# A causal attention with two gated MLPs on one core: when the planner ranks twelve small rows, and whether it holds small VectorE steps back for GpSimd

## The chip, the cores and the metric

The kernel runs on one core of one Trainium2 chip. The metric is the device time of one execution in microseconds (us); of several executions the median counts. Engines are called PE (TensorE), DVE (VectorE), ACT (ScalarE), POOL (GpSimd) and SP (SyncE, which here only issues DMAs).

## The reference, cut to what matters

Three stages in float32: an attention over 4 batches of 8 heads with 576 positions of 64 elements, and two gated MLPs ("MoE") over the 2304 tokens that come out of it. The first of these begins with an RMS normalisation.

```python
cum = np.cumsum(np.maximum(s, 0.0), axis=-1)
bias = -(cum[:, :, :, None] - cum[:, :, None, :])
scores = np.where(causal, -1e9, scale * q @ k.T + np.minimum(bias, 0.0))
attn = exp(scores - max) / (sum + 1e-09)
x = (attn @ v), heads side by side           # 2304 x 512
xn = x / sqrt(mean(x * x) + 1e-06) * rms_g
h = (silu(xn @ w_gate) * (xn @ w_val)) @ w_out     # 512 -> 1536 -> 512
out = (silu(h @ w2_gate) * (h @ w2_val)) @ w2_out
```

## The kernel before, in words

**A planner writes the order.** The program never issues an instruction when it meets it. Every operation is put down with `op(engine, ns, fn, r=, w=, pri=, later=, port=)`: engine, estimated duration, what it reads and writes, a rank and two options. `Plan.run` then plays the whole list through a model and gives each engine its order: of the operations ready at a time, the one with the lowest `pri` goes first. On the chip every engine works through its own queue strictly in that order, and waits where something it needs isn't there yet.

Two options matter here. `later=1000` makes an operation ready 1000 ns (in the model) after the engines' work that it depends on. `port=True`, on a DVE operation, models SBUF ports that DVE and GpSimd share: such an operation isn't started in the model while a GpSimd operation runs there, and the reverse (L203 and L236). These are rules of the plan; on the chip nothing but semaphores and the hardware holds an instruction back. In the model SP is busy 450 ns with a small DMA, and about 1500 ns with a 512 KB one.

**The early attention.** The first 256 positions (group "A") of batches 0 and 1 are computed first, as sixteen small units, one for each head (`EarlyUnit`, i = 0 to 15, called head 0 to head 15 below; the first eight are those of batch 0). A unit loads q and k of its head in one DMA of 128 KB (L879), its values in one of 64 KB (L891), multiplies q by k (L899), finds the least of each row on DVE (L690), takes the exponent on ACT (L701), transposes it (L917) and multiplies by the values (L927). The bias by the cumulated s is a matmul of its own for units 0 to 3 (L905). For units 4 to 15 it is an added row of k: a DMA of 1 KB (L884) copies one row of the cumulated s (`cumA`) below k in the unit's tile, `lq`. Two tiles with two halves each serve all sixteen, so unit i can load only when the scores of unit i - 4 are done. All three loads have rank i - 1000 and go through SP's queue.

In the same queue stand the weights of the first MLP: 512 KB for each half of a hidden block f (L434, `raw<-in_w_gv`), with rank -992 + 1.5 f. They are turned into two fp32r halves by ACT (L438, L445), DVE (L440, L449) and POOL (L446, L449).

**The early normalisations.** When all eight heads of a batch are in x, `normalise(..., split=False)` runs for its 256 tokens: squares on ACT (L958), their sums on PE (L965), then 20 small steps on DVE, each a line `step(...)` from L1020 to L1054: the division by the softmax's sums, the mean, an inverse root by three Newton rounds of three steps (L1035, L1037, L1038), and the factors' two halves. Each step needs the one before it. Two transposes (L1058), a copy (L1061) and four spreading matmuls (L1066) follow, then x is scaled (L1070), split (L1073, L1075), and the gate matmuls of the first MLP (L1086) can begin. These have a rank far behind (10,000), so that the planner uses them to fill PE wherever the attention has nothing ready. The later normalisations, of the rest of the batches, call the same function with `split=True`.

**Behind it** come the remaining attention (group "B" and batches 2 and 3), with the first MLP's matmuls between, and then the two output layers and the second MLP.

Of the kernel before, what the change touches and what calls it, by code (L numbers as in the profile page):

```python
# [40 lines left out]
PE, DVE, ACT, POOL, SP, NONE = "PE", "DVE", "ACT", "POOL", "SP", "NONE"  # L41
# [38 lines left out]
class Plan:  # L80
# [20 lines left out]
    def op(self, eng, ns, fn, r=(), w=(), pri=0.0, later=0, port=False, slow=0.0):  # L101

        n = len(self.ops)
        done = 0
        if eng == SP:  # L110
            took = ns / self.RATE
            ns = max(450.0, took)
            done = 2300.0 + took - ns + slow
        deps, shared = set(), []
        for accesses, writes in ((r, False), (w, True)):
            for a in accesses:
                buf, part = a if isinstance(a, tuple) else (a, None)
                key = buf if isinstance(buf, str) else buf.key
                live = self.live.setdefault(key, [])
                keep = []  # L120
                for part2, m, wrote in live:
                    meets = part is None or part2 is None or part == part2
                    if meets and (writes or wrote) and m != n:
                        deps.add(m)
                    if not (writes and meets and (part is None or part == part2)):
                        keep.append((part2, m, wrote))
                keep.append((part, n, writes))
                self.live[key] = keep
                if not isinstance(buf, str) and buf.share is not None and buf not in shared:
                    shared.append(buf)  # L130
                    buf.uses += 1
        engs = eng if isinstance(eng, list) else [(eng, ns)]
        self.ops.append((engs, fn, deps, pri, done, shared, later, port))
        return n
# [160 lines left out]
TINY = 70  # L295
# [5 lines left out]
def tile_kernel(  # L301
# [16 lines left out]
    op = plan.op  # L318
# [10 lines left out]
    def buf(pool, tag, shape, dtype, name=None):  # L329
        return Buf(f"{pool}.{tag}",  # L330
                   lambda: pools[pool][1].tile(shape, dtype, name=name or tag, tag=tag))
# [143 lines left out]
    cumA = buf("at", "pTB1", [P, 2 * P], F32, "cumA")  # L475
# [100 lines left out]
    class Head:  # L576
# [13 lines left out]
        def load(self, pri):  # L590
            b, h, n, nv = self.b, self.h, self.n, self.nv
            i = b * NH + h
            c0 = self.c0
            q0, k0, c0_ = lq_parts(self.ql, 0)
            q1, k1, c1_ = lq_parts(self.ql, 1)
            self.qp, self.kp = [k0, k1], [q0, q1, c0_, c1_]
            op(SP, 4 * P * n, lambda en: en.dma_start(
                out=self.ql()[:, :n], in_=qk[b, h, :, 1, :n]), w=self.kp, pri=pri, later=2500)
            op(SP, 4 * D * (QW - c0), lambda en: en.dma_start(
                out=self.ql()[:D, S + c0:], in_=qk[b, h, :D, 0, c0:]),  # L600
               w=self.qp, pri=pri, later=2500)
            op(SP, 4 * P * n, lambda en: en.dma_start(
                out=self.cb()[:, :n], in_=cum_d[i:i + 1, :n].to_broadcast([P, n])),
               r=["cum_d"], w=[self.cb], pri=pri, later=2500)
            op(SP, 256 * P * nv, lambda en: en.dma_start(out=self.vl()[:, :nv], in_=vp[b, h, :, :nv]),
               w=[self.vl], pri=pri, later=2500)
# [241 lines left out]
    class EarlyUnit(Unit):  # L848
# [28 lines left out]
        def load(self, pri):  # L877
            ql, i = self.ql
            op(SP, 8 * D * 256, lambda en: en.dma_start(  # L879
                out=ql()[0:D, :, 288 * i:288 * i + 256], in_=qk[self.b, self.h, 0:D, :, 0:256]),  # L880
               w=self.parts[:2], pri=pri)
            n = self.b * NH + self.h
            if not self.first:
                op(SP, 1024, lambda en: en.dma_start(  # L884
                    out=ql()[D:D + 1, 1, 288 * i:288 * i + 256], in_=cumA()[n:n + 1]),
                   r=[cumA, self.rows], w=self.parts[2:], pri=pri, later=1000)
            if self.first:
                op(ACT, 450, lambda en: en.dma_start(
                    out=self.v(), in_=vp[self.b, self.h, :, 0:2]), w=[self.vl], pri=pri - 1e6)
            else:  # L890
                op(SP, 512 * P, lambda en: en.dma_start(  # L891
                    out=self.v(), in_=vp[self.b, self.h, :, 0:2]), w=[self.vl], pri=pri)
# [47 lines left out]
    def normalise(i, g, tot, pri, split=True):  # L940
# [15 lines left out]
        for k in range(KD):  # L956
# [3 lines left out]
               r=[(x, (k, 0)), (x, (k, 64))], w=[q], pri=pri)  # L960

            if not split:
# [14 lines left out]
                op=ALU.subtract), r=[q, qh], w=[sqL], pri=pri, port=True)  # L977
# [6 lines left out]
        if split:  # L984
# [3 lines left out]
               r=[ps], w=[sq[0]], pri=pri)  # L988
            ps2 = mo_bank()
            for c in range(nt):  # L990
                op(PE, C_TR, lambda en, c=c: en.transpose(
                    ps2()[:, c * P:c * P + P], sq[0]()[:, at[c]:at[c] + P], ident()),
                   r=[sq[0], ident], w=[ps2], pri=pri)
# [3 lines left out]

        def step(fn, r=(), w=None):
            w = [col] if w is None else w
            op(DVE, TINY, fn, r=[*w, *r], w=w, pri=pri, port=True)  # L1000

        def m():
            return col()[:, 0, :nt]
# [13 lines left out]
        def u():  # L1017
            return fac()[:, 1, :nt]
        F, U = (fac, 0), (fac, 1)
        step(lambda en: en.tensor_scalar(out=over(), in0=tot()[:, :nt], scalar1=1.0e-9,  # L1020
                                         scalar2=None, op0=ALU.add), [tot], [F])
        step(lambda en: en.reciprocal(over(), over()), [], [F])
        step(lambda en: en.tensor_tensor(out=u(), in0=squares(), in1=over(), op=ALU.mult),
             [ps, F], [U])
        step(lambda en: en.tensor_tensor(out=u(), in0=u(), in1=over(), op=ALU.mult), [F], [U])
        step(lambda en: en.tensor_reduce(out=m(), in_=u(), axis=mybir.AxisListType.X,
                                         op=ALU.add), [U])
# [6 lines left out]
        for _ in range(3):  # L1034
# [8 lines left out]
            op=ALU.mult), [col], [F])  # L1043
# [7 lines left out]
        def columns(z):  # L1051
# [3 lines left out]
                                         op=ALU.subtract), [F], [rr])  # L1055
        tp = mo_bank()
        for c in range(nt):
            op(PE, C_TR, lambda en, c=c: en.transpose(  # L1058
                tp()[:, at[c]:at[c] + P], rr()[:, c * P:c * P + P], ident()), r=[rr, ident], w=[tp],
               pri=pri)  # L1060
        op(ACT, c_act(n), lambda en: en.activation(rT(), tp()[:, :n], ACTF.Copy),  # L1061
           r=[tp], w=[last], pri=pri)
        for k in range(KD):
# [10 lines left out]
               r=halves, w=[(H, k)], pri=pri)  # L1074
            op([(POOL, c_ptt(n)), (DVE, c_tt(n))], 0, lambda en, k=k: en.tensor_tensor(  # L1075
                out=L()[:, k, :n], in0=x()[:, k, :n], in1=f32(H()[:, k, :n]), op=ALU.subtract),
               r=halves + [(H, k)], w=[(L, k)], pri=pri, port=True)
# [56 lines left out]
    later = setup()  # L1134
# [767 lines left out]
```

## Time and profile before

| | |
|---|---|
| median of 3 runs | 1056.55 us (1056.55, 1058.98, 1052.65) |
| profiled execution, device time | 1057.39 us |
| its span, first to last instruction | 1055.6 us |
| mean granted clock of PE, of full speed | 0.997 |
| PE busy | 1040.2 us (99%) |
| DVE, ACT, POOL busy | 771.7 (73%), 641.5 (61%), 273.5 us (26%) |

All stretches and rows are of that one profiled execution, and their times count from the start of its span; 1.8 us of the device time lie around the span. A share of busy time is an average over stages. PE's clock has two levels, 2.4 GHz (1.00) and 1.2 GHz (0.50).

### The profile page before, as it was taken

How to read it: one execution, taken by the hardware profiler on the slowest of the kernel's cores; microseconds unless marked ns; L12 is line 12 of the kernel's file. 1: busy time of each engine (PE TensorE's matmuls, PEld its weight loads, DVE VectorE, ACT ScalarE, POOL GpSimd, SP SyncE). 2: the span in 40 equal slices, each digit the busy share in tenths (PEclk: the TensorE clock that was granted, in tenths of full speed). 3: DMA queues.
4: the chain of work that ended last, by engine and by line, in shares of the span. 5: the costliest groups of instructions: out<-in, count | busy, mean ns of one | idle time of the engine just before them, and what ended most of it. 6: DMA issues, size and time to landing. Idle time of an engine off the chain costs nothing.

```text
span 1055.6 us, 19496 instructions
## 1 busy us (share of the span) xinstructions
PE 1040.2 (99%) x6322; PEld 937.2 (89%) x6322; DVE 771.7 (73%) x1880; ACT 641.5 (61%) x1373; POOL 273.5 (26%) x370
## 2 busy tenths in 40 slices
PE   8899999999999999999999999999999999999998
PEld 6599999999999999999988889888888888888888
DVE  7699788777777776757779887665667766976462
ACT  6689778867664775333466865555556444665652
POOL 4368556544343542000000000212122221300000
PEclk9899999999999999999999999999999999999999
DMA  7797555534546732666697662666667667888673
GB/s 204 229 282 221 144 150 148 164 117 128 158 142 204 246 106 85 188 208 206 206 299 244 197 222 84 222 210 220 228 202 256 219 232 263 292 259 261 207 244 105
DMA packets 127959, 211.17 MB, mean 200 GB/s; under 512 B 16176, under 2 KB 55600, under 8 KB 127856
## 3 DMA queue, kind: packets, MB, share of 16 engines
q1 hardware_dynamic: 126656, 209.32, 62.8%
q8 instruction: 50, 0.82, 0.3%
q10 hardware_dynamic: 1200, 0.60, 0.2%
q14 instruction: 53, 0.43, 0.1%
HBM read 145.29 MB, written 64.56 MB: 199 GB/s over the span
## 4 chain that ended last, share of the span: by engine, by line
PE 79%; DMA 7%; DVE 6%; ACT 3%; issue 3%; POOL 1%; SPq 1%; ACTq 0%; POOLq 0%; DVEq 0%
PE mo L1086 21%; PE mo L1455 8%; PE mo L1626 8%; PE sps L1626 6%; PE tp L1455 6%; PE sps L1455 5%; PE tp L745 4%; PE tp L733 3%; PE sps L664 2%; PE mo L1702 2%; DMA raw<-in_w_gv 2%; PE sps L1086 2%; PE tp L1086 2%; PE mo L1510 2%; DMA lq<-cumA 1%
## 5 line engine op out<-in xcount | busy, mean ns | idle before, releaser
L1086 PE MATMUL mo<-xL,H 128*128 128x256 f32 (+1 forms) x672 | 201.8, 300 | 0.1
L1086 PE MATMUL mo<-xH,H 128*128 128x256 f32 (+1 forms) x672 | 200.7, 300 | 0.3
L1086 PE MATMUL mo<-xH,L 128*128 128x256 f32 (+1 forms) x672 | 200.2, 298 | 0.0
L1351 DVE TENSOR_TENSOR hL<-hh,hH 128x512 fp32r<-128x512 f32 (+1 forms) x192 | 125.2, 662 | 67.1 <-ACT hH L1348 66.4
L1348 ACT ACTIVATE hH<-hh 128x512 fp32r<-128x512 f32 (+1 forms) x192 | 115.2, 603 | 91.6 <-DVE hL L1351 21.3
L1086 PEld LDWEIGHTS mo<-xL,H 128*128 128x128 f32 x672 | 127.0, 189 | 1.0 <-POOL xL L1075 0.5
L1086 PEld LDWEIGHTS mo<-xH,H 128*128 128x128 f32 x672 | 126.7, 189 | 1.1 <-ACT xH L1073 0.6
L1086 PEld LDWEIGHTS mo<-xH,L 128*128 128x128 f32 x672 | 126.9, 189 | 0.2
L701 ACT ACTIVATE sc<-sc,col 128x128 f32<-128x128 f32 (+3 forms) x128 | 73.2, 572 | 48.4 <-DVE col L690 46.1
L1455 PE MATMUL mo<-hH,wo 128*128 128x512 f32 x312 | 97.8, 389 | 0.0
L1455 PEld LDWEIGHTS mo<-hH,wo 128*128 128x128 f32 x312 | 58.6, 188 | 12.2
L1455 PE MATMUL mo<-hL,wo 128*128 128x512 f32 x156 | 61.1, 391 | 0.2 <-DVE hL L1351 0.2
L1455 PE MATMUL tp<-hH,wo 128*128 128x512 f32 x192 | 60.4, 389 | 0.0
L1093 ACT ACTIVATE t<-mo 128x256 f32<-128x256 f32 (+1 forms) x84 | 33.9, 403 | 43.4 <-PE mo L1086 43.3
L1632 ACT ACTIVATE u<-sps 128x512 f32<-128x512 f32 x48 | 28.5, 593 | 50.6 <-PE sps L1626 48.8
L745 PE MATMUL tp<-pTB,vst 128*128 128x320 f32 (+2 forms) x320 | 52.2, 294 | 1.6 <-ACT pTB L736 1.0
L1455 PE MATMUL sps<-hH,wo 128*128 128x512 f32 x168 | 52.9, 389 | 0.0
L1095 DVE SCALAR_TENSOR_TENSOR t<-t,mo 128x256 f32<-128x256 f32 (+1 forms) x84 | 37.8, 450 | 19.4 <-ACT t L1093 19.1
L738 DVE TENSOR_TENSOR pTB<-tp,pTB 128x512 fp32r<-128x512 f32 x64 | 44.0, 687 | 8.3 <-ACT pTB L736 7.2
L745 PEld LDWEIGHTS tp<-pTB,vst 128*128 128x128 f32 x320 | 46.5, 189 | 3.6 <-ACT pTB L736 1.7
L1589 POOL TENSOR_TENSOR tmp<-x,x 128x512 f32<-128x512 f32 x2 | 2.9, 1454 | 178.5 <-DVE x L1471 178.5
L733 PE MATMUL tp<-ident,sc 128*128 128x128 f32 x304 | 46.9, 274 | 0.6 <-DVE x L754 0.4
(289 smaller groups left out, 2925.9 us busy)
## 6 DMA issues: line engine op xcount, KB each, us to landing
raw<-in_w_gv SPq DMA_DIRECT2D x44, 511.8 KB, 5.4
tb<-h_d SPq DMA_DIRECT2D x48, 256.0 KB, 3.9
t<-tb SPq DMA_DIRECT2D x48, 256.0 KB, 2.4
hh<-t SPq DMA_DIRECT2D x48, 256.0 KB, 3.1
lq<-in_qk SPq DMA_DIRECT2D x32, 288.0 KB, 3.6
cb<-cum_d SPq DMA_DIRECT2D x32, 288.0 KB, 3.9
hh<-h_d SPq DMA_DIRECT2D x36, 256.0 KB, 3.6
h_d<-hh SPq DMA_DIRECT2D x54, 128.0 KB, 2.3
```

What stands on the lines that cost most here:

```text
L701: op(ACT, c_act(o + m, 2) + 35, lambda en: en.activation(sc()[:m, :o + m], sc()[:m, :o + m], ACTF.Exp, scale=-1.0, bias=col()[:m, 0, t:t + 1],
L733: op(PE, C_TR, lambda en, pt=pt, a=a, kb=kb, t=t: en.transpose(pt()[:, a * P:a * P + P], self.sc[t]()[:, kb * P:kb * P + P], ident()), r=[ ...
L738: op(DVE, c_tt(n), lambda en, pt=pt, c=c: en.tensor_tensor(out=place(L, c), in0=source(pt, c), in1=f32(place(H, c)), op=ALU.subtract), r=[ ...
L745: op(PE, c_mm(n), lambda en, w=w, z=z, kb=kb, d0=d0, n=n, o=o: en.matmul(po()[:, o:o + n], vst[j]()[:, kb, :], pT[g][z]()[:, d0:d0 + n], s ...
L1086: op(PE, c_mm(n), lambda en, a=a, x=x, c=c, k=k, i=i: en.matmul(ps()[:, :n], a()[:, c], x()[:, k, :n], start=(k == 0 and i == 0), stop=(k ...
L1093: op(ACT, c_act(n), lambda en: en.activation(t()[:, :n], gp()[:, :n], ACTF.Tanh, scale=0.5), r=[gp], w=[t], pri=pri)
L1095: op(DVE, c_tt(n), lambda en: en.scalar_tensor_tensor(out=t()[:, :n], in0=t()[:, :n], scalar=1.0, in1=gp()[:, :n], op0=ALU.add, op1=ALU.mu ...
L1348: op(ACT, c_act(n) + 35, lambda en: en.activation(H(), src(), ACTF.Copy), r=[src, *after], w=[H], pri=pri)
L1351: lambda en: en.tensor_tensor(out=L(), in0=src(), in1=f32(H()), op=ALU.subtract),
L1455: op(PE, c_mm(n), lambda en, m=m, w=w, xx=xx, kk=kk, i=i: en.matmul(ps[m]()[:, :n], w(), xx(), start=first and kk == 0 and i == 0, stop=kk ...
L1626: op(PE, c_mm(n), lambda en, w=w, xx=xx, cut=cut, kk=kk, i=i: en.matmul(ps()[:, :n], W[w]()[:, cut], xx(), start=first and kk == 0 and i == 0,
L1632: op(ACT, c_act(n), lambda en: en.activation(dst(), ps()[:, :n], ACTF.Copy), r=[ps], w=[dst], pri=-1.0e4)
```

## The change

Two lines. The row of the cumulated s gets a rank three lower than the other loads of its unit, so that in SP's queue it stands as the loads of the unit three before it do. The small steps of a normalisation are put down with `port=split`: for the two early ones, where `split` is False, the planner no longer keeps them and GpSimd's operations apart; for the others nothing changes. What is computed is the same.

```diff
@@ class EarlyUnit: load @@
             if not self.first:
                 op(SP, 1024, lambda en: en.dma_start(
                     out=ql()[D:D + 1, 1, 288 * i:288 * i + 256], in_=cumA()[n:n + 1]),
-                   r=[cumA, self.rows], w=self.parts[2:], pri=pri, later=1000)
+                   r=[cumA, self.rows], w=self.parts[2:], pri=pri - 3, later=1000)
@@ def normalise @@
         def step(fn, r=(), w=None):
             w = [col] if w is None else w
-            op(DVE, TINY, fn, r=[*w, *r], w=w, pri=pri, port=True)
+            op(DVE, TINY, fn, r=[*w, *r], w=w, pri=pri, port=split)
```

## Rows read from the trace of the kernel before

**Rows 1.** Waits of PE, first 90 us: total, times, longest (us).
```profile
PE sps L899 <- DMA lq<-cumA: 3.5, 2, 2.5
```

**Rows 2.** Stretches: length, then each engine's busy us (instructions), granted clock, DMA share, GB/s.
```profile
0.00:38.30 38.30, 32.08 (x178) 23.22 (x179) 28.12 (x111) 26.67 (x80) 15.93 (x31) 1.00 0.74 202
38.30:60.00 21.70, 20.55 (x117) 16.02 (x118) 16.43 (x47) 15.79 (x41) 7.30 (x8) 0.84 0.82 260
60.00:75.00 15.00, 14.69 (x116) 14.19 (x116) 13.96 (x48) 13.42 (x32) 11.77 (x13) 1.00 0.90 280
```

**Rows 3.** The same view, finer, around the longest wait (order: PE PEld DVE ACT POOL).
```profile
35.80:38.30 2.50, 0.03 (x1) 0.02 (x1) 0.63 (x2) 1.22 (x3) 1.48 (x2) 1.00 0.67 205
38.30:40.00 1.70, 1.69 (x7) 1.70 (x8) 0.30 (x2) 0.49 (x2) 0.00 (x0) 0.50 0.86 232
...
42.00:44.00 2.00, 2.00 (x9) 1.46 (x7) 0.77 (x4) 0.39 (x2) 1.90 (x2) 0.50 0.20 39
44.00:45.50 1.50, 1.50 (x6) 0.68 (x5) 0.43 (x2) 1.00 (x5) 0.04 (x1) 0.63 0.69 205
```

**Rows 4.** Timeline of SP's queue: start, us, line, what is issued.
```profile
28.82 0.57 SPq L434 DMA_DIRECT2D raw<-in_w_gv  x1
29.48 0.38 SPq L891 DMA_DIRECT2D vl<-in_vp  x1
29.91 0.43 SPq L434 DMA_DIRECT2D raw<-in_w_gv  x1
30.38 0.55 SPq L879 DMA_DIRECT2D lq<-in_qk  x1
31.33 0.33 SPq L891 DMA_DIRECT2D vl<-in_vp  x1
31.70 0.56 SPq L884 DMA_DIRECT2D lq<-cumA  x1
```

**Rows 5.** DMAs issued from 29.9 to 32.25 us: size, us to landing.
```profile
raw<-in_w_gv SPq DMA_DIRECT2D x1, 511.8 KB, 7.1
lq<-in_qk SPq DMA_DIRECT2D x1, 128.0 KB, 7.3
...
lq<-cumA SPq DMA_DIRECT2D x1, 1.0 KB, 6.5
```

**Rows 6.** Timeline of PE: start, us, line, tiles [idle before, releaser].
```profile
26.89 0.68 PE L899 MATMUL sps<-lq 128*128 128x256 f32 x2
...
30.43 0.86 PE L927 MATMUL tp<-pTA,vl 128*64 128x256 f32 x4
...
40.72 1.54 PE L927 MATMUL tp<-pTA,vl 128*64 128x256 f32 x4
...
46.68 0.86 PE L927 MATMUL tp<-pTA,vl 128*64 128x256 f32 x4 [0.65 <-DVE pTA L923]
...
51.24 0.57 PE L1086 MATMUL mo<-xH,H 128*128 128x256 f32 x2
52.31 0.44 PE L917 MATMUL tp<-ident,sc 128*128 128x128 f32 x2 [0.49 <-ACT sc L701]
```

**Rows 7.** Timeline of DVE: three small steps of the first normalisation.
```profile
30.22 0.17 DVE L1023 TENSOR_TENSOR fac<-mo,fac 128x16 f32<-128x16 f32 x1
...
35.10 0.16 DVE L1038 SCALAR_TENSOR_TENSOR rc<-rc 128x2 f32<-128x2 f32 x1
...
41.17 0.15 DVE L1035 SCALAR_TENSOR_TENSOR rc<-rc 128x2 f32<-128x2 f32 x1
```

**Rows 8.** Tile rc, first 95 us: duration in ns (least/median/most), first and last start.
```profile
L1037 DVE TENSOR_TENSOR rc<-rc x6: 142/156/973, 33.3 to 86.3; 128x2 f32<-128x2 f32 x6
L1038 DVE SCALAR_TENSOR_TENSOR rc<-rc x6: 148/162/835, 33.5 to 86.6; 128x2 f32<-128x2 f32 x6
...
L1028 DVE TENSOR_SCALAR rc<-rc x2: 155/700/1245, 32.0 to 66.7; 128x2 f32<-128x2 f32 x2
```

**Rows 9.** The same view of tile fac.
```profile
L1054 DVE TENSOR_TENSOR sq<-fac,sq x2: 177/224/270, 48.1 to 91.1; 128x16 f32<-128x16 f32 x2
```

## The prediction

> **What bounds the kernel now.** I read the share of busy time first: TensorE (PE) is busy 1040.2 of 1055.6 us, so only its 15.4 us of idle time, and stretches at a low granted clock, can be won. Next the table of stretches [rows 2]: 6.2 us of that idle time lie before 38.3 us, 1.15 between 38.3 and 60, 0.3 between 60 and 75. Both edits touch work that ends by 91.4 us (the last small step, L1054 [rows 9]), so what lies behind can change only because the planner orders it anew.
>
> Then the waits of PE [rows 1]: the longest in the first 90 us, 3.5 us in two pieces, ends with a row of the cumulated s landing (lq<-cumA); the larger piece is 2.5 us. The stretches around it [rows 3] show PE busy 0.03 of 2.5 us up to 38.3, and then the granted clock at 0.50 (1.2 GHz instead of 2.4) until 44 and 0.63 on average until 45.5, which puts the rise near 45.1. The smaller piece, 1.0 us, was followed by no fall: in the table the clock before 38.3 is 1.00.
>
> So one stall costs twice. What the clock costs: 6.8 us at half speed would lose 3.4 us if all work followed the clock; four value matmuls (L927) took 1.54 us at the low clock against 0.86 at the full one [rows 6], which makes it 6.8 x (1 - 0.86/1.54) = 3.0. I take 3.2. Stall and clock together are 5.7 us, 0.54% of the time.
>
> **Edit 1, the row ranked three heads ahead.** No DMA is added: 12 rows (heads 4 to 15 of the first sixteen) change their place in SP's queue. Each needs the cumulated s, long there, and the scores of the head four before it; in the planner it is ready 1000 ns after those. The two late rows differ.
>
> Head 4's (the 1.0 us piece): its old rank, -996, already beat the weight transfer issued before it (-990.5), so only its ready time put it behind, and the new rank alters nothing there. Gain 0.
>
> Head 13's: SP's order [rows 4] is weight half at 28.82, values of head 11, weight half at 29.91, q and k of head 13 at 30.38, values of head 12 at 31.33, the row at 31.70. Head 9's scores end at 27.5 (26.89 + 0.68 [rows 6]), so on that clock the row is ready near 28.6, before the second weight half. The old rank, -987, stands behind that half (-987.5) and both values (-989, -988); the new one, -990, beats all three. I expect it at about 29.4, in front of 512 KB of weights, and landed near 33, about as the transfers issued before it.
>
> But the scores of head 13 need its q and k too, and these keep rank -987. They were issued at 30.38 and landed 7.3 us later, at 37.7; the row landed at 31.70 + 6.5 = 38.2 [rows 5]. Between them lie only 0.5 us. With the row out of the way the next late one is this 128 KB transfer, behind the same two weight halves. The stall shrinks from 2.5 to 2.0 us, not to nothing: gain 0.5. The bounds: all of it, 2.5, if the new order also puts q and k before the second half; 0, if SP's 450 ns for the row let the values of head 12 become ready first. They outrank q and k and wait until 31.3 for head 8's value matmuls (30.43 + 0.86 [rows 6]); q and k would then be issued where the row is now and land near 38.2. I take 0.5, the difference of the two landings as they stand.
>
> Displaced in SP's queue are values of heads up to three back, by one issue (0.55 us). Head 11's are issued at 29.48 and used at 40.72 [rows 4, 6], so this is hidden; the cover is some 7 us and ends only if a value transfer slips behind two more weight halves.
>
> The clock: an idle time of 1.0 us left it at 2.4 GHz, one of 2.5 us was followed by 1.2. The 2.0 us that I expect to remain lie between, nearer to the fall. Bounds 0 and 3.2; I take a third of the price, 1.1, because the executions shown before differ by 6.3 us (1052.65 to 1058.98), so that a step of this size may be absent in some already.
>
> **Edit 2, the small steps.** An early normalisation has 20 steps on VectorE (DVE). The planner set one only where GpSimd (POOL) was idle in the plan; now it doesn't look. No instruction is added.
>
> First normalisation: 12 steps from L1023 at 30.22 to the end of the second Newton round at 35.26 take 5.0 us, 0.42 each with other work between; the next comes only at 41.17 [rows 7], the last at 48.1 (L1054 [rows 9]), since in that order they stand behind GpSimd's conversions and behind head 13's scores. Unheld, the six left would take 6 x 0.42 = 2.5 us and end near 37.8 to 38. From the last step to the first gate matmul (L1086, 51.24) are 3.2 us, so the MoE's matmuls could start near 41 instead of 51 and fill gaps behind that: 0.65 us before the value matmuls at 46.68 and 0.49 at 52.31 [rows 6]. Sum 1.1. All idle time from 38.3 to 75 is 1.15 + 0.3 = 1.45, the upper bound; the lower is a loss (third rival). They come too late for the stall itself: it begins at 35.8, before the chain ends, and PE takes its instructions in order.
>
> Second normalisation: its 18 steps from L1023 on fall after 60, where PE is busy 14.69 of 15 us and DVE 13.96 [rows 2]. To end earlier frees more MoE work there, and little is idle: gain 0.
>
> The Trainium skill has a rule against this edit (SBUF — State Buffer, "Who interferes with whom"): a DVE operation in a two-port mode, or with two SBUF inputs against a GpSimd operation that reads SBUF, fully blocks until the one that came first is done. The trace agrees: L1028 took 1245 ns at worst against 155 at best [rows 8].
>
> **The sum.** 1057.4 (the profiled execution) - 0.5 - 1.1 - 1.1 = 1054.7. The median of the runs shown lies 0.8 below that execution, so as a median 1053.9; own range of this case 1051.5 to 1056.5. A kernel of this spread can't tell 0.5% (5.3 us) from no change, so this case is "the same".
>
> **Rivals.**
> 1. The stall goes entirely, clock and all: 1057.4 - 2.5 - 3.2 - 1.1 = 1050.6, as a median 1049.8. For it: 2.5 us less at the head of a chain that PE follows for the next 7 us. Against it: q and k landing at 37.7. Needed is that the new plan lifts these over a weight half too, or that early MoE matmuls come into PE's order before head 13's scores. Chance 0.2.
> 2. The row doesn't move, or q and k take its late place: only the filled gaps remain, 1057.4 - 1.1 = 1056.3, median 1055.5. For it: a margin of SP's order of about one issue. Chance 0.2.
> 3. Slower: the second normalisation's steps meet GpSimd on its ports. Between 60 and 75 GpSimd is busy 11.77 of 15 us, 78% [rows 2]. Three steps there already ran 1.09, 0.81 and 0.67 us over their best (L1028, L1037, L1038 [rows 8]), 2.6 together. Packed into that stretch, 18 steps x 0.78 x half of 1.09 us make 7.7, that is 5.1 more (bounds: 0, and 18 x 1.09 = 19.6). DVE has 15 - 13.96 = 1.0 us free, so 4.1 us fall on its other work, the scores' minima and weight conversions. It decides only where PE runs out of MoE matmuls whose weights are converted. If all reaches PE and nothing of edit 1 is won: 1057.4 + 4.1 = 1061.5, median 1060.7. Against it: PE's 0.3 us of idle time there shows work in store. Chance 0.13.
>
> **How the numbers follow.** Forecast 0.47, rivals 0.2, 0.2, 0.13. Faster by over 0.5% (below 1051.3): three quarters of rival 1 and a tenth of the forecast and of rival 2, 0.22. Slower by over 0.5% (above 1061.8): half of rival 3 and a little of rival 2, where a new order of all later work goes badly, 0.09. The same: 0.69. The range goes from rival 1's time to rival 3's, 1049.6 to 1060.5.
>
> **What would show it.** Head 13's row issued before the weight half and landed by 34, and PE's wait before head 13's scores ending with lq<-in_qk instead of lq<-cumA, near 37.7: step 1 right. A wait that still ends with the row, or no wait, shows it wrong. A granted clock of 1.00 all through 38 to 46, and the gain nears rival 1. L1054 before 39 and the first L1086 before 43 show edit 2 right; small steps over 1 us in number, with PE waiting for DVE after 60, show rival 3. What would make the whole wrong: a new wait behind 100 us, where the order changes too without my having priced it.

## The result: 0.8% slower, where 0.25% faster was forecast

| | before | after |
|---|---|---|
| median of 6 runs each | 1054.17 us (1052.41 to 1058.98) | 1063.93 us (1061.26 to 1065.93) |
| ratio | | 1.0082, 95% interval 1.0056 to 1.0107 |
| profiled execution, its span | 1057.39, 1055.6 us | 1065.05, 1063.3 us |
| PE busy, idle in the span | 1040.2, 15.4 us | 1043.7, 19.6 us |

The three runs added on the side of before pulled its median down by 2.4 us: the profile that the prediction was read from is one of its slower executions. Of the 7.7 us between the two spans, 4.2 are idle time of PE; the other 3.5 are busy time for the same 6322 matmuls, so idle time, which the rows below go by, is not the whole loss. Times below are ratios to runs of the kernel before on the same chip, since its median moved between 1053 and 1056 us from one set of runs to another.

**The early stall.** After: waits of PE up to 100 us (total, times, longest), where [rows 1] had 3.5 us ending with the row.

```profile
PE sps L899 <- DMA vl<-in_vp: 2.6, 2, 2.1
PE sps L664 <- DVE rc L1035: 1.3, 1, 1.3
...
PE mo L1066 <- DVE hh L1098: 1.0, 1, 1.0
PE sps L899 <- DMA lq<-in_qk: 0.6, 1, 0.6
...
PE mo L1058 <- DVE sq L1054: 0.5, 1, 0.5
```

SP's queue after, as in [rows 4] (start, us, line, what is issued):

```profile
31.13 0.43 SPq L434 DMA_DIRECT2D raw<-in_w_gv  x1
31.66 0.55 SPq L884 DMA_DIRECT2D lq<-cumA  x1
32.31 0.53 SPq L891 DMA_DIRECT2D vl<-in_vp  x1
32.88 0.42 SPq L434 DMA_DIRECT2D raw<-in_w_gv  x1
33.40 0.50 SPq L884 DMA_DIRECT2D lq<-cumA  x1
33.99 0.53 SPq L891 DMA_DIRECT2D vl<-in_vp  x1
34.58 1.25 SPq L879 DMA_DIRECT2D lq<-in_qk  x2
```

Counted from head 4, the row at 31.66 is head 13's and the first transfer at 34.58 its q and k. The row now stands ahead of a weight half, with four other issues between it and its own q and k. It is issued at 31.66, as late as before (31.70), and lands some 3 us earlier, near 35.3; q and k land 5.0 us behind their issue (7.3 in [rows 5]). DMAs issued from 31.6 to 32.25 us, and from 34.5 to 35.9 (the second line is of two transfers):

```profile
lq<-cumA SPq DMA_DIRECT2D x1, 1.0 KB, 3.6
lq<-in_qk SPq DMA_DIRECT2D x2, 128.0 KB, 5.0
```

PE's wait before head 13's scores ends with q and k:

```profile
15.11 0.46 PE L899 MATMUL sps<-lq 128*128 128x128 f32 x2 [2.08 <-DMA vl<-in_vp]
...
39.79 0.89 PE L899 MATMUL sps<-lq 128*128 128x128 f32 x4 [0.62 <-DMA lq<-in_qk]
...
44.86 0.42 PE L1086 MATMUL mo<-xH,H 128*128 128x256 f32 x2
```

That is PE's timeline, as in [rows 6]. The wait is 0.62 us where [rows 3] had 2.5, and the first gate matmul starts at 44.86 instead of 51.24. But head 13's scores start 1.5 us later than before (39.79, against 38.31 where the wait of [rows 3] ends): PE comes late to the place, after a wait of 2.08 us for head 4 and a fall of the granted clock behind that, from 16.0 to 19.4 us (third line). At the old place the clock stays up (stretches as in [rows 3]):

```profile
35.80:38.30 2.50, 2.29 (x14) 1.31 (x12) 2.30 (x13) 2.16 (x7) 0.31 (x1) 1.00 0.92 255
38.30:40.00 1.70, 1.08 (x10) 1.02 (x10) 1.67 (x6) 1.59 (x4) 1.62 (x2) 1.00 0.98 261
17.00:19.00 2.00, 2.00 (x7) 1.48 (x6) 0.91 (x5) 1.50 (x6) 0.25 (x1) 0.50 0.15 36
```

**Where the time went instead.** The same three stretches of three profiles, in this order: before, after, and a second execution of the kernel before (b2 below). First number: length; second: PE busy.

```profile
0.00:55.00 55.00, 47.62 (x258) 34.70 (x258) 39.95 (x150) 37.51 (x110) 20.91 (x36) 0.94 0.76 221
55.00:110.00 55.00, 54.35 (x427) 52.57 (x426) 51.78 (x160) 49.67 (x118) 42.65 (x52) 1.00 0.79 245
110.00:235.00 125.00, 124.81 (x953) 123.20 (x953) 99.03 (x364) 95.17 (x242) 69.11 (x111) 1.00 0.49 142
```

```profile
0.00:55.00 55.00, 49.73 (x284) 37.71 (x285) 42.20 (x149) 40.71 (x118) 21.80 (x40) 0.97 0.77 223
55.00:110.00 55.00, 51.47 (x395) 49.09 (x394) 51.17 (x148) 46.32 (x106) 38.08 (x47) 1.00 0.77 235
110.00:235.00 125.00, 122.15 (x916) 118.74 (x916) 101.30 (x352) 93.07 (x234) 62.17 (x103) 1.00 0.49 136
```

```profile
0.00:55.00 55.00, 49.49 (x287) 36.94 (x288) 44.45 (x156) 41.29 (x118) 22.31 (x38) 1.00 0.81 235
55.00:110.00 55.00, 54.30 (x430) 53.13 (x430) 51.06 (x165) 47.43 (x114) 42.35 (x54) 1.00 0.80 240
110.00:235.00 125.00, 124.81 (x952) 123.37 (x951) 97.76 (x357) 95.86 (x244) 67.87 (x110) 1.00 0.50 144
```

Up to 55 us the changed kernel is ahead of the first profile of before (284 matmuls to 258), but not of the second (287). From 55 to 235 PE is idle 3.53 + 2.85 = 6.4 us after, 0.84 and 0.89 before. The instruction counts say it again: between 110 and 235 PE got through 916 matmuls instead of 953. The part between 60 and 75 us that [rows 2] showed nearly full has PE busy 12.17 of 15 us now:

```profile
60.00:75.00 15.00, 12.17 (x91) 11.38 (x91) 14.76 (x49) 10.71 (x26) 9.76 (x12) 1.00 0.79 260
```

There the second normalisation's steps stand close together. DVE after (start, us, line):

```profile
60.39 1.06 DVE L1030 TENSOR_SCALAR rc<-rc 128x2 int32<-128x2 int32 x1
...
61.74 1.22 DVE L1032 TENSOR_SCALAR rc<-rc 128x2 int32<-128x2 int32 x1
...
65.19 1.08 DVE L1038 SCALAR_TENSOR_TENSOR rc<-rc 128x2 f32<-128x2 f32 x1
66.19 0.34 DVE L690 CUSTOM_DVE_ANT_0 sc<-sps,sc,col 128x128 f32<-128x128 f32 x1
66.46 0.08 DVE L690 DVE_READ_ACCUMULATOR2_ANT col<- 128x1 f32 x1
66.46 0.15 DVE L1035 SCALAR_TENSOR_TENSOR rc<-rc 128x2 f32<-128x2 f32 x1
```

and GpSimd's operation there, and PE behind them:

```profile
64.95 1.30 POOL L449 TENSOR_TENSOR L<-raw,H 128x512 fp32r<-128x512 f32 x1 [2.02 <-ACT H L445]
...
66.69 0.41 PE L664 MATMUL sps<-kHH,qst 128*128 128x384 f32 x1 [1.34 <-DVE rc L1035]
```

The reader is to see one chain: GpSimd is at work from 64.95 to 66.25 (L449), so L1038 takes 1.08 us instead of the 0.16 of [rows 8]; the minimum of the scores (L690) stands behind it in DVE's queue, and PE's next scores wait for that. (The row names L1035 as the releaser, which ends 0.07 us behind the minimum. In the program the scores write the tile `sps`, which the minimum reads, and touch nothing of `rc`; that they waited for the minimum is inferred from this.) L1054, at 91.1 before [rows 9], runs at 69.35.

Behind 110 us nothing of the edits is left, and yet PE waits (after; the same stretch of both profiles of before lists no wait):

```profile
PE tp L745 <- DVE pTB L738: 1.9, 3, 1.3
PE sps L664 <- DVE col L690: 0.5, 1, 0.5
PE mo L1086 <- POOL xL L1075: 0.2, 1, 0.2
```

### The profile page after: what moved, and what is told of

Same layout as the page of the kernel before. It is cut to its first block, busy times and chain, and to the rows that moved or that the text cites. A ratio compares the mean times of both kernels' runs of the same rounds, so it can differ in the third digit from the quotient of the medians.

```text
span 1063.3 us, 19489 instructions
## 1 busy us (share of the span) xinstructions
PE 1043.7 (98%) x6322; PEld 937.8 (88%) x6322; DVE 784.8 (74%) x1879; ACT 644.0 (61%) x1378; POOL 265.5 (25%) x366
## 4 chain that ended last, share of the span: by engine, by line
PE 58%; DMA 9%; DVE 7%; issue 3%; SPq 2%; ACT 2%; POOL 1%; ACTq 0%; DVEq 0%; POOLq 0%
PE mo L1086 15%; PE mo L1455 8%; PE mo L1626 6%; PE sps L1626 5%; PE sps L1455 4%; PE tp L1455 4%; DMA raw<-in_w_gv 3%; PE tp L745 2%; DMA tb<-h_d 2%; PE sps L1086 2%; PE tp L1086 2%; PE mo L1702 2%; PE tp L733 2%; PE mo L1510 2%; PE sps L664 1%
```

## The experiments

Three theories. A: the second normalisation's packed small steps cost the time, where DVE is full. B: the rows, early in SP's queue, delay other loads. C: neither; the planner writes a wholly new order from some 25 us on, and a new order costs a few us by itself, whatever brought it about.

**One edit at a time, and half of the second.**

```diff
 e1:  pri=pri  ->  pri=pri - 3     (rows only; steps port=True)
 e2:  port=True  ->  port=split    (steps only; rows pri=pri)
 e3:  pri=pri - 3,  port=split or i == 1     (rows, steps of the first normalisation)
 e4:  pri=pri - 3,  port=split or i == 0     (rows, steps of the second normalisation)
```

> Only the row's rank is changed (edit 1); the small steps are planned as before. Theory A (the second normalisation's small steps, packed into the stretch from 60 to 75 us where DVE is full, cost the time): 1051 to 1056 us, no loss. Theory B (the rows, now in front of their own q and k in SP's queue, delay loads and weights): about 1060 to 1064. Theory C (no single culprit; any new order of the later work costs or wins a few us): anywhere between 1050 and 1062, and the pieces don't add up.

> Only the small steps are planned without regard to GpSimd (edit 2), the rows keep their rank. Theory A: 1060 to 1064 us, the whole loss. Theory B: 1052 to 1056, about the kernel before. Theory C: anywhere between 1050 and 1062.

> Both edits, but the small steps only of the first early normalisation (batch 0); those of the second are planned as before. Theory A: 1051 to 1056 us, the loss is gone, while the first gate matmul still starts near 45 us. Theory B: about 1062. Theory C: anywhere between 1050 and 1062.

> Both edits, but the small steps only of the second early normalisation (batch 1); those of the first are planned as before. Theory A: 1060 to 1066 us, the loss stays. Theory B: about 1062 too. Theory C: anywhere between 1050 and 1066, on no particular side of the run with the first normalisation alone.

Measured: e1 1.0078 (1.0052 to 1.0104), e2 1.0082 (1.0054 to 1.0109), e3 1.0032 (1.0012 to 1.0052), e4 1.0149 (1.0112 to 1.0187). Either edit alone loses what both together lose, so the pieces don't add up: A missed e1, B missed e2 and e3. (A's ranges for e2 and e3 were missed too, by 0.3 and 0.6 us.) C held as far as it goes, e4 aside, which lies above its 1066 in time (1068.9). Part of e4's excess is the clock: its four executions had mean granted clocks of 0.990 to 0.998, those of e1 0.998 to 1.000. At 0.998 e4 took 1064.5 us and e1 1061.6. In e4 and e2, which share the second normalisation's packed steps, PE waits once, for 2.9 and 2.4 us, for DVE; this row is of e4 (its waits of PE):

```profile
PE sps L664 <- DVE col L690: 2.9, 1, 2.9
```

**New orders with neither edit, and the kernel before once more.** Each is one constant of the planner, of which the chip knows nothing:

```diff
 n1:  RATE = 350.0  ->  RATE = 351.0       n4:  RATE = 349.0
 n2:  SLACK = 1500.0  ->  SLACK = 1510.0
 n3:  TINY = 70  ->  TINY = 80
 b2:  nothing
```

> The kernel before with neither edit; only the planner's rate for DMAs is 351 instead of 350 bytes per ns, which changes no work but makes it write another order from some 25 us on. Theory C (the written order of before is better than what the planner gives on the average; any new order loses a few us, most of it between 110 and 235 us): 1055 to 1060 us, with 2 to 5 us lost to the kernel before between 110 and 235 us. Theory A (only the packed small steps of the second normalisation cost) and theory B (only the rows cost): 1051 to 1055, as before.

> The kernel before with neither edit; only the planner's SLACK is 1510 instead of 1500, another order from about 45 us on. Theory C: 1055 to 1060 us, most of the loss between 110 and 235 us. Theories A and B: 1051 to 1055.

> The kernel before with neither edit; only the planned duration of a small step is 80 instead of 70 ns, and it is still kept apart from GpSimd. Theory C: 1055 to 1060 us, most of the loss between 110 and 235 us. Theories A and B: 1051 to 1055.

> The kernel before once more, for a second profile: does head 13's stall, with the fall of the clock behind it, belong to every execution? If it does: PE waits 2.5 us there and the granted clock falls to 0.50, time about 1057. If not: a smaller wait, no fall, and a time 3 us lower, near the median of 1053. No theory hangs on it but the size of what there was to win.

> Neither edit; the planner's DMA rate 349 instead of 350. Theory C (any new order loses): 1055 to 1064 us. If the written order of before is only average among its like: as likely below 1054 as above.

Measured: n1 1.0062 (1.0039 to 1.0085), n2 1.0011 (0.9990 to 1.0033), n3 1.0087 (1.0060 to 1.0113), n4 1.0010 (0.9978 to 1.0042). Of four orders without any edit one (n3) loses what the change did, one (n1) three quarters of it, and none wins; n2 and n4 can't be told from the kernel before. n1 and n3, at 1061.8 and 1065.1 us, lie even above what C expected. n3 keeps the steps apart from GpSimd and leaves the rows alone, and has the same kind of waits between 55 and 110 us (waits of PE, n3):

```profile
PE sps L664 <- DVE col L793: 1.8, 1, 1.8
PE tp L745 <- DVE pTB L819: 1.5, 1, 1.5
PE mo L1086 <- DVE x L1070: 1.2, 1, 1.2
```

n4 gives PE nearly the old order: set beside that of before by line and tile, as the traces have it, PE's order of its 6322 matmuls differs in 70 lines, against 674 to 1014 for the other three. In its stretches PE is as busy as before:

```profile
55.00:110.00 55.00, 54.55 (x431) 53.17 (x431) 51.71 (x163) 50.08 (x118) 41.88 (x51) 1.00 0.83 258
110.00:235.00 125.00, 124.82 (x956) 123.23 (x956) 99.22 (x361) 95.24 (x240) 67.67 (x111) 1.00 0.49 140
```

So C is shown for its first half: an order may lose 0.9% with neither edit. Its place was named too narrowly: in n3 PE is idle for 5.8 us between 55 and 110 and for 2.2 between 110 and 235, in n1 for 2.7 and 2.1.

b2 ran 1053.24 us. Head 13's wait is 1.2 us there, and no fall of the clock follows it (stretches of b2, to be laid beside [rows 3]):

```profile
35.80:38.30 2.50, 1.30 (x10) 1.08 (x11) 1.34 (x6) 1.23 (x3) 1.91 (x2) 1.00 1.05 262
38.30:40.00 1.70, 1.70 (x10) 1.04 (x10) 1.17 (x5) 1.11 (x5) 0.00 (x0) 1.00 0.80 260
```

The stall and fall that the prediction priced at 5.7 us were, in this execution of the same program, 1.2. The first gate matmul, too, starts at 47.3 us here, 3.9 earlier than in the first profile.

**Pairs: both edits in those orders.**

```diff
 m1, m2, m3, m4 = the changed kernel with the constant of n1, n2, n3, n4
```

> Both edits, and the planner's DMA rate 351 instead of 350: the pair of the run with that rate alone (1061.8 us). Theory C (orders differ by several us whatever the edit is; the loss of both edits is one such draw): between 1055 and 1066, no worse than its pair on the average of the three pairs. Theory A (the edits themselves cost about 8 us): about 8 us above its pair, 1068 to 1072.

> Both edits, and the planner's SLACK 1510 instead of 1500: the pair of the run with that slack alone (1057.0 us). Theory C: between 1055 and 1066, on the average of the three pairs within 4 us of them. Theory A: about 1065.

> Both edits, and the planned duration of a small step 80 instead of 70 ns: the pair of the run with that duration alone (1065.1 us). Theory C: between 1055 and 1066. Theory A: about 1073.

> Both edits and the rate 349: the pair of the run with that rate alone. Theory C: on the average over the four pairs within 4 us. Theory A (the edits themselves cost 8 us): 8 us above its pair.

| constant | neither edit | both edits | difference |
|---|---|---|---|
| RATE 351 | 1.0062 | 1.0052 | -0.10% |
| SLACK 1510 | 1.0011 | 1.0084 | +0.73% |
| TINY 80 | 1.0087 | 1.0087 | 0.00% |
| RATE 349 | 1.0010 | 1.0052 | +0.42% |
| mean | 1.0043 | 1.0069 | +0.26% |

The differences scatter by 0.38%, so the mean is known to +-0.6% only: the edits' own cost, on the average over orders, may be nothing or nearly the whole 0.8%. A's 0.8% in each pair is refuted by m1 and m3.

**The steps left out on the chip.** The changed kernel's order is kept to the instruction, but 11 steps of the second normalisation issue nothing:

```diff
-        def step(fn, r=(), w=None):
+        def step(fn, r=(), w=None, keep=True):
...
-            op(DVE, TINY, fn, r=[*w, *r], w=w, pri=pri, port=split)
+            op(DVE, TINY, fn if keep or split or i == 0 else lambda en: None, r=[*w, *r], w=w, pri=pri, port=split)
...
 (keep=False on L1028, L1032 and the three lines of the Newton rounds)
```

> The changed kernel in exactly its own order, but 11 of the 18 small steps of the second early normalisation (L1028, L1032 and the three Newton rounds) are left out on the chip, so its factors are not the reference's. Two of the four steps that GpSimd held for about 1 us are among them (L1032, L1038). If the packed steps make DVE late and PE with it: PE's wait of 1.3 us near 65 us gone, 2 to 4 us less than the changed kernel, 1060 to 1062. If DVE is full there anyway and the steps only show it: within 1 us of it, 1063 to 1065. In neither case is the kernel before (1054) reached under theory C.

Measured 1.0066 (1.0041 to 1.0092), 1061.62 us: in the range of the first answer, but the interval overlaps the changed kernel's, so in time it is inconclusive. The profile is plainer: the wait of 1.3 us at L664 and that of 0.5 at L1058 are gone, and PE's idle time from 55 to 110 us falls from 3.53 to 2.32 (its busy time in this row of s1):

```profile
55.00:110.00 55.00, 52.68 (x406) 50.23 (x405) 51.91 (x145) 47.84 (x111) 39.03 (x50) 1.00 0.78 238
```

Part of what a held step cost is then paid by the next DVE instruction on the ports (DVE of s1):

```profile
59.08 1.13 DVE L1030 TENSOR_SCALAR rc<-rc 128x2 int32<-128x2 int32 x1
...
60.50 1.75 DVE L440 SCALAR_TENSOR_TENSOR raw<-raw,cvy 128x512 uint32<-128x512 uint32 x1
```

L440 takes 0.69 us in the median. GpSimd is at work meanwhile:

```profile
60.83 0.86 POOL L628 TENSOR_TENSOR vst<-vl,vst 128x320 fp32r<-128x320 f32 x1
```

DVE stays full with 11 steps fewer: 51.91 of 55 us.

**The first normalisation's steps alone.** They had looked like a gain: e3 is 0.46% under e1, the changed kernel 0.67% under e4.

```diff
 f1:  port=True  ->  port=split or i == 1
 f2:  the same, and SLACK = 1510.0
```

> Rows as before; only the first early normalisation's small steps are planned without regard to GpSimd. If their gain, 4 to 7 us where they were added to the rows, belongs to the edit: 1048 to 1051 us, faster than the kernel before. Theory C: the new order eats it, 1053 to 1060, while the first gate matmul still starts near 42 us.

> The same with the planner's SLACK at 1510, whose time without the edit is 1057.0 us. If the gain belongs to the edit: 1050 to 1053. Theory C: anywhere between 1053 and 1062.

Measured: f1 1.0068 (1.0036 to 1.0100), f2 1.0044 (1.0020 to 1.0068) against n2's 1.0011. f1, at 1063.6 us, lies above even what C expected. Its first gate matmul does start early, at 42.5 us; the time is lost later, 4.9 us of PE idle between 55 and 110 and 1.9 between 110 and 235. The same edit wins 0.46 and 0.67% in two orders (the second against e4 and its low clocks) and loses 0.68 and 0.33% in two others: its sign belongs to the order. No version beat the kernel before, so there is none to recommend.

**All orders side by side**, idle time of PE from 55 to 235 us in each profile, and the ratio:

| | idle, us | ratio | | idle, us | ratio |
|---|---|---|---|---|---|
| before | 0.84 | 1 | n1 | 4.82 | 1.0062 |
| n4 | 0.63 | 1.0010 | e2 | 5.08 | 1.0082 |
| e3 | 2.38 | 1.0032 | m4 | 5.46 | 1.0052 |
| n2 | 2.87 | 1.0011 | m1 | 5.53 | 1.0052 |
| m3 | 3.30 | 1.0087 | f2 | 5.53 | 1.0044 |
| e1 | 4.26 | 1.0078 | after | 6.38 | 1.0082 |
| m2 | 4.38 | 1.0084 | f1 | 6.88 | 1.0068 |
| | | | e4 | 7.46 | 1.0149 |
| | | | n3 | 8.01 | 1.0087 |

The correlation over the 16 is 0.75. About half of the spread of the ratios goes with this one stretch, the first MLP's matmuls between attention units, where DVE is busy for 89 to 95% of the time from 55 to 110 us.

## Why the prediction was wrong, point by point

- **The failed step: what lies behind the edits was priced at nothing.** The first paragraph said that it "can change only because the planner orders it anew", the sum had no term for that, and the last sentence left "a new wait behind 100 us" unpriced. The four orders without edits put the term at 0.10 to 0.87% of the time, 0.43% on the average; two of the four are losses clear of the noise, and none is a gain. That is half of the change's 0.82% and larger than any term of the sum. How much of the 0.82% is order alone, and how much the edits, the pairs don't settle.
- **Edit 1.** Right: head 13's row moved ahead of the weight half, and the wait then ended with q and k. Wrong: the row was issued at 31.66 instead of 29.4 and landed near 35.3, not by 34. Wrong in size: 0.6 us remained instead of 2.0, since q and k landed near 39.7 instead of 37.7, but PE came 3.3 us later (it was idle before head 13's scores from 39.17 on, and from 35.8 before). That the wait shrank further than forecast is thus no gain, but PE's lateness. Head 4's wait, held to be untouched, was 2.08 us after (it begins at 13.03), 1.05 and 1.13 in the profiles of before, 1.71 in s1 with the changed order. How much of that is order and how much chance isn't settled.
- **The clock, -1.1.** b2 shows a wait of 1.2 us and no fall of the clock behind it in the same program, so the term rested on one execution. The sign that was named for a gain near rival 1, a clock of 1.00 from 38 to 46, came true, and yet the kernel lost: its fall had come at 16.0 us instead, behind the 2.08 us wait. Over all executions nothing was won from the clock either: the mean granted clock is 0.997 in the six after, and in the 28 executions of the kernel before that were timed with n4. The doubt was in the text (the runs' spread of 6.3 us); it should have led to nothing from this term, not a third.
- **Edit 2, first normalisation, -1.1.** The mechanism was right for the steps: L1054 moved from 48.1 to 39.1 (forecast: before 39). The first gate matmul moved from 51.24 to 44.86 (forecast: before 43), 5.7 us behind L1054 instead of some 3; against b2's 47.3 only 2.4 us of that are the change's. The gain wasn't kept: PE's lead of 26 matmuls at 55 us (284 to 258; none against b2) is a lag of 6 at 110 (679 to 685), while DVE, busy 14.76 of 15 us from 60 to 75, is what PE waits for there. The cover that hid the second normalisation, MoE work "in store", is not in store in the place where PE's order needs it: PE waited in order at L664, L1058 and L1066.
- **Edit 2, second normalisation, 0.** This is rival 3, given 0.13, and in part it did happen: priced at 4.1 us, it would have to be found in the 2.9 us more idle time between 55 and 110, of which 1.2 went when s1 left steps out; n3 has more idle time there with these steps kept apart. Adding these steps cost 0.71% (e1 to e4), 0.50% (e3 to after) and 0.14% (f1 to e2, within the intervals). That the medians have one sign shows little: e4 ran at lower clocks than e1, and where the clock was 1.000, e2 (1058.4 to 1059.7) lies below f1 (1060.2 to 1063.6). Not as priced: single steps were not held more than before in sum (four of about 1.1 us now, more of smaller size before [rows 8]); they were held close together, in 10.7 us from L1023 on instead of some 30.
- The range ended at 1060.5 (rival 3's own sum gives 1060.7). It took the rivals' terms but no width for the order itself; four orders without edits alone spread over 8 us.

Open: why the order of before leaves PE so little idle time from 55 to 235 us. Nothing run here shows a cause; that n4, the nearest to it on PE, keeps this, fits.

## What to carry to other kernels

Where a planner writes the whole order, an edit to one rank is an edit to everything behind it: first time a few orders that differ by a planner's constant alone, and put their spread into the range before any mechanism is priced. Judge a part of such a change by pairs over several orders, not by one kernel against one kernel. And take a second profile before a stall is priced: the size of the one here, and the fall of the clock behind it, differed between two executions of one program.

## What the runs showed of the hardware that was not expected

- The same program waited 2.5 us at head 13 with the clock at 0.50 for 6.8 us behind it, and in another execution 1.2 us with the clock at 1.00 throughout that place. Idle times of 1.05, 1.13 and 1.2 us were followed by no fall in the profiles of before.
- The length of the wait alone doesn't tell: 2.36 us (e2, at 60.8) and 2.14 us (e4, at 38.2) were followed by no fall, 2.08 us (after) by one at 16.0, and in b2 the clock fell at 324.3 us behind a wait of 0.55 that ended at 322.8 (granted clock 0.57 on average from 324 to 328):

```profile
322.00:324.00 2.00, 1.45 (x6) 0.63 (x5) 2.00 (x6) 1.24 (x4) 0.74 (x2) 1.00 0.77 285
324.00:328.00 4.00, 3.86 (x18) 3.67 (x19) 2.80 (x7) 2.59 (x6) 4.00 (x5) 0.57 0.44 143
```

- Much of the scatter of one program is the clock. Of the 28 executions of the kernel before that were timed with n4, the seven with a mean granted clock of 0.999 or 1.000 took 1050.7 to 1055.2 us, the four with 0.994 or less 1059.1 to 1061.9. The losses of n1 and n3 are not of this kind: at 0.998 they took 1061 to 1063 and 1063 to 1066 us, the kernel before 1053 to 1057.
- Leaving out an operation that GpSimd holds can pass the delay on: with L1032 left out, the next conversion (L440) took 1.75 us instead of 0.69. This is the lock of the shared ports that the prediction quoted from the Trainium skill (SBUF — State Buffer, "Who interferes with whom"); the runs add that leaving out a held step needn't give its time back.
